# A linear-attention and balanced-expert kernel: the first units in another order, gate weights later in the load queue, and one expert's weight sums behind an addition

## The chip, the cores and the metric

The kernel runs on one NeuronCore of a Trainium2 chip. The metric is the device time of one execution in microseconds (us). Before the change the median of six runs is 411.55 us, from 409.94 to 413.15.

The engines are named as in the profile: PE is TensorE (PEld its weight loads), DVE is VectorE, ACT is ScalarE, POOL is GpSimd, and SP is SyncE, which here only issues transfers.

## The reference

Two blocks follow each other. The first is a linear attention with a decaying state, over 4 sequences, 8 heads, 768 steps and a head size of 48:

```python
for t in range(S):
    kt, vt, rt = (k[:, :, t], v[:, :, t], r[:, :, t])
    cur = np.einsum('bhd,bhe->bhde', u[None] * kt, vt)
    y[:, :, t] = np.einsum('bhd,bhde->bhe', rt, state + cur)
    state = w[None, :, :, None] * state + np.einsum('bhd,bhe->bhde', kt, vt)
```

Its output, as 3072 rows of 384, goes into a layer of 8 experts. Pairs of a token and an expert are taken in falling order of their logits; a pair counts if the token is still free and the expert has fewer than 384 tokens. Each token then goes through its one expert:

```python
logits = x @ w_gate
...
for e in range(E):
    mask = assigned == e
    h = np.maximum(x[mask] @ w1[e], 0.0)      # w1[e]: 384 x 1024
    out[mask] = h @ w2[e]                     # w2[e]: 1024 x 384
```

## The kernel before, in words

**Attention.** The 24 units are pairs of a sequence and a chunk of 128 steps, in chunk order. A unit loads three tensors of 192 KB (`load`, L426: keys `kt`, receptances `rt`, values `vt`), each as 192-byte rows, through SP's queue. Then, for each unit: POOL multiplies `rt` by `kt` and by `u` (`step_products`, L445 and L446); DVE sums that per head into `dd` (`own`, L449), and scales the keys by a table of powers of the decay, `wk`, into `ks` (`scale`, L435); PE transposes receptances and keys (`rows_turned` L461, `keys_turned` L472); DVE scales the turned receptances out of PSUM (`receptances`, L466) and ACT copies the turned keys (L474); PE forms the products of all pairs of steps (`pairs`, L522). The matrix `AT` of a head has `dd` on its diagonal, written by ACT as the identity times a column of `dd` (`diagonal`, L454, one instruction for each of 8 heads), and DVE writes the products above the diagonal over it, under a mask (L524). PE then makes the state's share (L540), the state's update (L550), and the output from `AT` and the values (L567); ACT copies the output (L571). After every fourth unit PE forms the logits (L584), which need the gate weights `wg_sb`.

The first chunk (units 0 to 3) has no state share. Tables and the first two units are made in `Mild.__init__`, ahead of a branch: if all decays lie in a range, `attention_mild` runs, else `attention_any`, which does not run for these inputs. The order of PE, DVE, ACT and POOL there is the order of the code (`manual_schedule`), and inside `attention_mild` that of SP too. So a step that waits holds all later ones of its engine. `wait(n)` (L353) issues products of the identity that nobody reads.

POOL, DVE and PE also carry small constants for the search in the gaps of the units: `constants()` is a generator, and from unit 3 on three of its steps run in each unit.

**Experts.** For each expert a search on DVE, with counts on PE, finds the 384 tokens; POOL gathers their rows (L1238), SP loads `w1` and `w2` (1.5 MB each; L1229, L1284). If the search fails, a longer one (`surely`) runs in a branch at L939; it does not run here. PE forms the hidden layer (L1328), the last 128 rows of the result directly (`result`, L1386), and the first 256 rows by seven products in place of eight (`results`, L1407). For these, DVE makes four sums of quarters of `w2` (`halves_of`, T0 to T3, L1374) and four sums of the hidden layer (L1397 to L1400). The seven products leave PSUM through DVE: `both`, `low`, the second row block's right half (L1422), `high`, then L1426, L1427 and L1430. PSUM has two banks for these products, so the fourth group, p4, waits until `high` has read the second.

In the experts the scheduler of the compiler orders DVE, by its own model of times. With `issue_after(x)` a block's instructions come behind `x` on its engine.

Of the kernel before, what the change touches and what calls it, by code (L numbers as in the profile page):

```python
# [285 lines left out]
class Mild:  # L286
# [6 lines left out]
    def __init__(self, ctx, tc, r, k, v, w, u, wg, ident):  # L293
# [36 lines left out]
        self.load(2)  # L330
        self.wg_sb = const.tile([128, HP, 32], F32, name="wg_sb")
        nc.gpsimd.memset(self.wg_sb, 0.0)
        for i in range(2):
            for j in range(2):
                nc.sync.dma_start(self.wg_sb[i * PD:i * PD + D, j::2, 0:E],
                                  wg.rearrange("(g i j d) e -> i j d g e", i=2, j=2, d=D)[i, j])
        self.load(3)

        self.state = [const.tile([128, HP, PD], F32, name=f"state{b}") for b in range(B)]
# [6 lines left out]
        with part, tc.manual_schedule(engines={nc.tensor.engine, nc.vector.engine, nc.scalar.engine, nc.gpsimd.engine}):  # L346
            awake = part.enter_context(tc.tile_pool(name="m_awake", bufs=1, space=PSUM)).tile([128, 3, 128], F32,
                                                                                              name="awake")

            def wait(n):  # L350

                for _ in range(n):
                    nc.tensor.matmul(awake, ident, ident.unsqueeze(1).to_broadcast([128, 3, 128]),  # L353
                                     start=True, stop=True)


            wait(1)
            row = row.rearrange("p h d -> p (h d)")
            w_ps = ps.tile([128, HP], F32, name="w_ps", tag="kT_ps")
            for a in range(HP):  # L360
                nc.tensor.transpose(w_ps[:, a:a + 1], row[:, ts(a, 128)], ident[0:1, 0:1])
            wait(2)
            wp = const.tile([128, 8, 2, HP], F32, name="wp")
            pw = tab.tile([128, 2, HP, M + 2], F32, name="pw")
            nc.vector.memset(pw[:, :, :, 0:1], 1.0)
            ones = tab.tile([128, 1], F32, name="ones")
            nc.vector.memset(ones, 1.0)

            nc.vector.tensor_scalar(out=wp[:, 0, 0, :], in0=w_ps, scalar1=W_MIN, scalar2=W_MAX,
                                    op0=ALU.max, op1=ALU.min)  # L370
            nc.vector.reciprocal(wp[:, 0, 1, :], wp[:, 0, 0, :])
            for j in range(7):
                n = 1 << j
                m = min(2 * n, M + 2) - n
                by = wp[:, j, :, :].unsqueeze(3).to_broadcast([128, 2, HP, m])
                nc.vector.tensor_mul(pw[:, :, :, n:n + m], pw[:, :, :, 0:m], by)
                nc.vector.tensor_mul(wp[:, j + 1, :, :], wp[:, j, :, :], wp[:, j, :, :])
            self.w_chunk = wp[:, 7, 0, :]

            ch = tab.tile([128, HP, T], F32, name="ch")  # L380
            nc.scalar.copy(ch[:, :, 0:M + 1], pw[:, 0, :, M::-1])
            nc.gpsimd.tensor_copy(ch[:, :, M + 1:T], pw[:, 1, :, 1:T - M])
            self.wr = const.tile([128, HP, T], F32, name="wr")
            nc.scalar.copy(self.wr[:, :, 0:M + 1], pw[:, 1, :, M + 1:0:-1])

            within = tab.tile([128, HP], F32, name="within")
            nc.vector.tensor_tensor(out=within, in0=wp[:, 0, 0, :], in1=w_ps, op=ALU.is_equal)
            nc.vector.tensor_copy(self.wr[:, :, M + 1:T], pw[:, 0, :, 0:T - M - 1])
            self.rows_turned(0)
            wait(1)  # L390
            sc_ps = ps.tile([128, HP, 128], F32, name="sc_ps", tag="kT_ps")
            for a in range(HP):
                nc.tensor.transpose(sc_ps[:, a, :], ch[:, a, :], ident)
            n_ps = awake[0:1, 0, 0:HP]
            nc.tensor.matmul(n_ps, ones, within, start=True, stop=True)
            n_within = tab.tile([1, 1], F32, name="n_within")
            nc.vector.tensor_reduce(out=n_within, in_=n_ps, axis=AX.X, op=ALU.add)
            flag = const.tile([1, 1], I32, name="flag")
            nc.vector.tensor_single_scalar(out=flag, in_=n_within, scalar=float(H * PD), op=ALU.is_equal)
            self.wk = const.tile([128, DX], F32, name="wk")  # L400
            nc.scalar.copy(self.wk.rearrange("p (h d) -> p h d", h=H),
                           sc_ps.rearrange("p a (q d) -> p (a q) d", q=2)[:, :, 0:D])
            self.step_products(0)
            self.receptances(0)
            self.rows_turned(1)
            wait(1)
            self.scale(0)
            self.own(0)
            self.diagonal(0, 0, 2)
            self.keys_turned(0)  # L410
            self.diagonal(0, 2)
            self.step_products(1)
            self.scale(1)
            self.receptances(1)
            self.keys_turned(1)
            self.own(1)
            self.holds = nc.values_load(flag[0:1, 0:1])

    def load(self, n):
# [28 lines left out]
    def own(self, n):  # L448
        self.tc.nc.vector.tensor_reduce(out=self.live[n]["dd"], in_=self.live[n]["rk"], axis=AX.X, op=ALU.add)  # L449

    def diagonal(self, n, first=0, end=None):
        AT, dd = self.live[n]["AT"], self.live[n]["dd"]
        for h in range(first, end or self.r.shape[1]):
            self.tc.nc.scalar.activation(AT[:, h % 2, h // 2, :], self.ident, AF.Copy, scale=dd[:, h:h + 1])  # L454

    def rows_turned(self, n):
# [20 lines left out]
def attention_mild(ctx, tc, mild, r, k, v, w, u, wg, x_dram, LG, ident, walk, first):  # L477
# [141 lines left out]
    search = walk.constants()  # L619
    with tc.manual_schedule(engines={nc.tensor.engine, nc.scalar.engine}):  # L620
        with tc.manual_schedule(engines={nc.vector.engine, nc.gpsimd.engine, nc.sync.engine}):

            nc.tensor.matmul(kv_ps, state[0][:, 0:2, :].rearrange("p a d -> p (a d)"),
                             ident.unsqueeze(1).to_broadcast([128, HP, T]), start=True, stop=True)
            mild.step_products(2)
            mild.scale(2)
            pairs(0)
            mild.diagonal(1)
            mild.own(2)
            for n in range(N):  # L630
                if n + 2 < N:
# [4 lines left out]
                    mild.scale(n + 3)  # L636
                    mild.step_products(n + 3)
                if n + 2 < N:
                    mild.diagonal(n + 2, 0, 4)
                if n + 1 < N:  # L640
                    pairs(n + 1)
                if n > 0 and n % B == 0:
                    logits(n // B - 1)
                if n + 2 < N:
                    mild.diagonal(n + 2, 4)
                from_state(n)
                new_state(n)
                if n > 0 and n % B == 0:
# [35 lines left out]
class Assignment:  # L684
# [26 lines left out]
    def __init__(self, ctx, tc, ML, CAP):  # L711
# [29 lines left out]
        new("own_lo", [128, 1])  # L741
        new("iota_lo", [128, 128], I32)
        new("digits", [128, ND], I32)
        new("steps", [128, 8, ND], I32)
        new("top", [128, ND], I32)
        new("taken", [128, NT])
        new("last", [128, 1])

# [6 lines left out]
    def constants(self):  # L755
# [69 lines left out]
        yield  # L825

        nc.gpsimd.iota(self.digits, pattern=[[1, ND]], base=1, channel_multiplier=0)
        yield
        for g in range(8):
            nc.vector.tensor_single_scalar(out=self.steps[:, g, :], in_=self.digits, scalar=28 - 4 * g,  # L830
                                           op=ALU.logical_shift_left)
            yield

        nc.vector.tensor_single_scalar(out=self.top[:, 0:7], in_=self.steps[:, 0, 0:7], scalar=-1,
                                       op=ALU.bitwise_xor)
        yield
        nc.vector.tensor_single_scalar(out=self.top[:, 7:ND - 1], in_=self.steps[:, 0, 7:ND - 1],
                                       scalar=-2147483648, op=ALU.bitwise_xor)
        yield
        nc.vector.tensor_copy(self.top[:, ND - 1:ND], self.top[:, ND - 2:ND - 1])  # L840
        yield
        nc.gpsimd.memset(self.taken, 0.0)
        yield
# [202 lines left out]
    def surely(self, pool, fmax, acc, place):  # L1046
# [11 lines left out]
        prop = pool.tile([128, NT, E], BF16, name="prop")  # L1058
        tt(prop, self.by_expert(self.first_e), self.by_token(em), ALU.is_equal)


        cand, bits = self.top, None
        for g in range(8):
            all_ps = self.count(pool, m, prop, cand.bitcast(F32), self.digit_15)
            most = pool.tile([128, ND], F32, name="most")
# [14 lines left out]
            if g < 7:  # L1080

                base = pool.tile([128, ND], I32, name="base")
                tt(base, self.steps[:, g + 1, :], flip.to_broadcast([128, ND]), ALU.bitwise_xor)
                cand = pool.tile([128, ND], I32, name="cand")
                nc.vector.scalar_tensor_tensor(out=cand, in0=dg.to_broadcast([128, ND]), scalar=28 - 4 * g,
                                               in1=base, op0=ALU.logical_shift_left, op1=ALU.bitwise_xor)
# [102 lines left out]
def rwkv5_eagle_then_base_layer_balanced(  # L1189
# [202 lines left out]
    def results(n, hid, weights, tok, turn):  # L1392
# [16 lines left out]

        def sum_of(product, other, name):  # L1410
            out = spool.tile([128, HX], F32, name=name)
            nc.vector.tensor_add(out, product, other)  # L1412
            return out

        out = [opool.tile([128, DX], F32, name="o_sb") for _ in range(2)]
        p1, p6 = pair((A[0][0], B[0][0]), (S[1], T[1]))
        one = spool.tile([128, HX], F32, name="one")
# [11 lines left out]
        p4, = pair((A[1][1], T[3]))  # L1429
        nc.vector.tensor_add(out[1][:, 0:HX], p4, low)  # L1430
        store(n, 1, out[1], tok)
        return xT


    awake = ps_t.tile([128, KD, 128], F32, name="xT_ps")
# [3 lines left out]
    for n in range(E):  # L1439
# [9 lines left out]

            ahead = following(n + 2 == E, chain(opening(hid, at, xT), result(n, 2, hid, at["w2"], at["tok"])), late)  # L1450
        else:
            weights_2 = halves_of(at["w2"])
            walk.behind = hidden(hid, 0, at["w1"], xT)
            if n + 1 < E:
                ahead = following(n + 2 == E)
# [1 line left out]
                hidden(hid, j, at["w1"], xT)  # L1457
            for _ in result(n, 2, hid, at["w2"], at["tok"]):
                pass
        xT = results(n, hid, weights_2, at["tok"], lambda: turn(ahead["xg"]) if n + 1 < E else None)  # L1460


# [26 lines left out]
```

## Time and profile before

| | |
|---|---|
| median of 6 runs | 411.55 us |
| profiled execution, time | 412.63 us |
| profiled execution, span of the trace | 410.9 us |
| granted PE clock over the span | 0.998 |
| PE busy | 392.5 us (96%) |
| DVE busy | 264.6 us (64%) |
| ACT busy | 148.2 us (36%) |
| POOL busy | 116.1 us (28%) |

The profiled execution took 412.63 us, 1.7 us more than the span that the trace covers and 1.1 us more than the median. The stages in the trace: tables and the first units' preparation to about 16 us, the units of the attention to 114 us, the last logits, the first search and the first loads to about 142 us, and the eight experts to the end. A line of the timeline gives start and duration in us, engine, line, operation, output and inputs, shape and count; behind it, in brackets, how long the engine was idle before and what ended that.

### The profile page before, as it was taken

The page shows a single profiled execution, that of the slowest core. Times are in us where ns is not written, and L with a number is a line of the kernel's source. Part 1 is how long each engine was busy: PE and PEld are TensorE (multiplying, and loading weights), DVE is VectorE, ACT ScalarE, POOL GpSimd, SP SyncE. Part 2 cuts the span into 40 slices and gives each one's busy share as a digit, 9 for nine tenths or more (in the row PEclk, how much of TensorE's full clock was granted, in tenths as well). Part 3 has the DMA queues.
Part 4 walks back from the last instruction along what each step waited for, and adds up shares of the span by engine and source line. Part 5 has one row for each costly group of instructions (what it writes and reads, how often), then busy time and mean ns, then how long its engine had stood idle before and what let it go on. Part 6 is the DMA issues. An engine that isn't in the chain of part 4 may idle for free. (4 is left out here: it accounts for less than half of the span.)

```text
span 410.9 us, 8511 instructions
## 1 busy us (share of the span) xinstructions
PE 392.5 (96%) x3174; PEld 289.7 (70%) x3174; DVE 264.6 (64%) x777; ACT 148.2 (36%) x382; POOL 116.1 (28%) x154
## 2 busy tenths in 40 slices
PE   7899999999997899989999999999999999999993
PEld 4588888888876495855785685595586577587583
DVE  5798879998568358478568658856856837421021
ACT  3798878778746021202112112121121211202200
POOL 5564964556200201210420320211112032201001
PEclk9999999999999999999999999999999999999999
DMA  9999999740029564712820830641461488201001
GB/s 148 168 173 183 180 177 172 144 76 2 3 78 345 184 230 158 230 38 53 295 77 3 273 125 25 206 180 39 172 213 40 140 304 288 57 21 38 0 21 38
DMA packets 93996, 54.43 MB, mean 132 GB/s; under 512 B 76784, under 2 KB 88176, under 8 KB 93936
## 3 DMA queue, kind: packets, MB, share of 16 engines
q1 hardware_dynamic: 89280, 41.70, 41.0%
q0 software_dynamic: 3072, 9.44, 6.9%
q10 hardware_dynamic: 1584, 2.56, 1.8%
q8 instruction: 29, 0.48, 0.5%
q14 instruction: 31, 0.25, 0.2%
HBM read 44.25 MB, written 9.44 MB: 131 GB/s over the span
## 5 line engine op out<-in xcount | busy, mean ns | idle before, releaser
L1328 PE MATMUL h_ps<-xT,w 128*128 128x384 f32 (+1 forms) x372 | 121.8, 475 | 0.0
L1328 PEld LDWEIGHTS h_ps<-xT,w 128*128 128x128 f32 x372 | 64.6, 190 | 35.9 <-issue 4.0
L1335 ACT ACTIVATE hid<-h_ps 128x384 f32<-128x384 f32 x56 | 27.5, 490 | 115.4 <-PE h_ps L1328 101.9
L1238 POOL DMA_INDIRECT xg<-x_rows,tok x24 | 24.9, 1039 | 144.0 <-issue 121.0
L454 ACT ACTIVATE AT<-ident,dd 128x128 f32<-128x128 f32 x192 | 59.4, 391 | 2.3 <-DVE dd L449 2.3
L1378 POOL DMA_INDIRECT out_dram<-o_sb,tok x24 | 25.9, 1078 | 106.0 <-DVE o_sb L1427 55.4
L1386 PE MATMUL o_ps<-w,hid 128*128 128x384 f32 x128 | 44.4, 493 | 0.9
L524 DVE COPY_PREDICATED AT<-mask,g_ps 128x512 f32<-128x512 uint8 x48 | 32.5, 729 | 8.2 <-PE g_ps L522 8.2
L1386 PEld LDWEIGHTS o_ps<-w,hid 128*128 128x128 f32 x128 | 23.5, 190 | 18.5 <-issue 4.4
L1407 PE MATMUL o_ps<-T,S 128*128 128x192 f32 x192 | 32.5, 326 | 0.0
L1407 PEld LDWEIGHTS o_ps<-T,S 128*128 128x128 f32 x192 | 31.4, 190 | 0.0
L522 PE MATMUL g_ps<-rT,kT 48*128 48x128 f32 x384 | 28.4, 285 | 0.1
L445 POOL TENSOR_TENSOR rk<-rt,kt 128x384 f32<-128x384 f32 x24 | 24.8, 1035 | 8.6 <-DMA rt<-in_r_dram 5.4
L522 PEld LDWEIGHTS g_ps<-rT,kT 48*128 48x128 f32 x384 | 23.6, 187 | 4.9 <-issue 2.9
L446 POOL TENSOR_TENSOR rk<-rk,u_bc 128x384 f32<-128x384 f32 x24 | 26.4, 1099 | 1.9
L567 PE MATMUL y_ps<-AT,vt 128*64 128x128 f32 x368 | 24.6, 276 | 0.0
L1407 PE MATMUL o_ps<-w,hid 128*128 128x192 f32 x128 | 24.6, 326 | 0.0
L1318 ACT COPY xT<-xT_ps 128x384 f32<-128x384 f32 x24 | 10.8, 481 | 34.3 <-PE xT_ps L1317 24.9
L1407 PEld LDWEIGHTS o_ps<-w,hid 128*128 128x128 f32 x128 | 20.9, 190 | 2.1
L1412 DVE TENSOR_TENSOR both<-o_ps,one 128x192 f32<-128x192 f32 x8 | 2.9, 358 | 27.8 <-ACT one L1418 27.8
L567 PEld LDWEIGHTS y_ps<-AT,vt 128*64 128x64 f32 x368 | 19.7, 137 | 0.9 <-issue 0.3
L466 DVE TENSOR_TENSOR rT<-rT_ps,wr 128x512 f32<-128x512 f32 x24 | 16.4, 683 | 5.3 <-PE rT_ps L461 5.2
(240 smaller groups left out, 591.9 us busy)
## 6 DMA issues: line engine op xcount, KB each, us to landing
w<-in_moe_w_dram SPq DMA_DIRECT2D x14, 1536.0 KB, 7.2
kt<-in_k_dram SPq DMA_DIRECT2D x24, 192.0 KB, 4.2
rt<-in_r_dram SPq DMA_DIRECT2D x24, 192.0 KB, 4.8
vt<-in_v_dram SPq DMA_DIRECT2D x24, 192.0 KB, 4.6
x_rows<-AT SPq DMA_DIRECT2D x8, 192.0 KB, 2.9
w<-in_moe_w_dram ACTq DMA_DIRECT2D x1, 1536.0 KB
x_rows<-rt SPq DMA_DIRECT2D x6, 192.0 KB, 2.3
x_rows<-ks SPq DMA_DIRECT2D x5, 192.0 KB, 2.2
```

Of the source, the lines that this page charges most:

```text
L445: nc.gpsimd.tensor_mul(rk, rt[:, :, 0:D], kt)
L446: nc.gpsimd.tensor_mul(rk, rk, self.u_bc.rearrange("p (h d) -> p h d", h=H))
L454: self.tc.nc.scalar.activation(AT[:, h % 2, h // 2, :], self.ident, AF.Copy, scale=dd[:, h:h + 1])
L522: nc.tensor.matmul(g_pss[q][:, a, :], kT[heads[q], a, :], rT[heads[q], a, :], start=True, stop=True)
L524: nc.vector.copy_predicated(out=AT[:, q], mask=mask.unsqueeze(1).to_broadcast([128, HP, T]), data=g_pss[q])
L567: nc.tensor.matmul(y[j][halves[i], g, :], vt[:, 2 * a + j, :], AT[:, j, a, :], start=(c == 0 and g == 0), stop=(g == 1), skip_group_check= ...
L1238: nc.gpsimd.indirect_dma_start(out=xg[:, c, :], out_offset=None, in_=x_dram, in_offset=bass.IndirectOffsetOnAxis(ap=tok[:, c:c + 1], axis=0))
L1328: product = nc.tensor.matmul(h_ps[:, cols], w1[:, f, ts(j, 128)], xT[:, f, cols], start=(f == 0), stop=(f == KD - 1))
L1335: nc.scalar.activation(hid[:, j, :], h_ps, AF.Relu)
L1378: nc.gpsimd.indirect_dma_start(out=out_rows[n * NC + c], out_offset=bass.IndirectOffsetOnAxis(ap=tok[:, c:c + 1], axis=0), in_=o_sb, in_of ...
L1386: nc.tensor.matmul(o_ps, hid[:, j, ts(c, 128)], w2[:, j, :], start=(j == 0), stop=(j == KF - 1))
L1407: nc.tensor.matmul(part, a[:, j, :], b[:, j, :], start=(j == 0), stop=(j == HF - 1))
```

## The change

1. The four transfers of the gate weights (L335) are issued behind the loads of units 4 and 5, and so behind those of units 0 to 5, where they stood behind those of units 0 to 2.
2. In the preparation, one filler ahead of the table's transposes (L390) goes. Receptances of unit 0 come ahead of the flag's two small DVE steps. A filler stands behind the flag's product. Keys of unit 0 are turned ahead of the rows of unit 1. Of unit 0's eight diagonals ACT writes the four of even heads, two before and two after the keys of unit 1; the four of odd heads are written by one DVE product of the identity and `dd`.
3. In `attention_mild` the pairs of unit 0 come ahead of the filler into `kv_ps` (L623) and not behind it.
4. Eleven small DVE steps that make `steps` and `top` go from `constants()` into `surely`.
5. The four sums of the second expert's `w2` are put behind `high` of the first expert.

```diff
@@ Mild.__init__
-        for i in range(2):
-            for j in range(2):
-                nc.sync.dma_start(self.wg_sb[...], wg...)
         self.load(3)
...
             self.rows_turned(0)
-            wait(1)
             sc_ps = ...                      # four transposes of ch
             nc.tensor.matmul(n_ps, ones, within, start=True, stop=True)
-            n_within = ...; flag = ...
             self.wk = ...                    # ACT copy of sc_ps
             self.step_products(0)
             self.receptances(0)
+            n_within = ...; flag = ...
+            wait(1)
+            self.scale(0)
+            self.keys_turned(0)
+            self.own(0)
             self.rows_turned(1)
             wait(1)
-            self.scale(0)
-            self.own(0)
-            self.diagonal(0, 0, 2)
-            self.keys_turned(0)
-            self.diagonal(0, 2)
             self.step_products(1)
             self.scale(1)
+            self.diagonal(0, range(0, H // 2, 2))
             self.receptances(1)
             self.keys_turned(1)
+            self.diagonal(0, range(H // 2, H, 2))
+            live = self.live[0]
+            nc.vector.tensor_mul(live["AT"][:, 1], ident.unsqueeze(1).to_broadcast([128, HP, T]),
+                                 live["dd"][:, 1::2].unsqueeze(2).to_broadcast([128, HP, T]))
             self.own(1)
+            for i in range(2):
+                for j in range(2):
+                    nc.sync.dma_start(self.wg_sb[...], wg...)
@@ attention_mild
-            nc.tensor.matmul(kv_ps, ...)     # the filler
             mild.step_products(2)
             mild.scale(2)
             pairs(0)
+            nc.tensor.matmul(kv_ps, ...)
             mild.diagonal(1, range(H))
@@ Assignment.constants -> Assignment.surely
-        for g in range(8):
-            nc.vector.tensor_single_scalar(out=self.steps[:, g, :], ...)
-        ...                                  # and three steps for top
@@ results / the experts' loop
-            nc.vector.tensor_add(out, product, other)
+            added.append(nc.vector.tensor_add(out, product, other).ins)
...
-            weights_2 = halves_of(at["w2"])
+            with ExitStack() as order:
+                if n == 1:
+                    order.enter_context(tc.issue_after(added))
+                weights_2 = halves_of(at["w2"])
...
-        xT = results(n, hid, weights_2, ...)
+        xT, added = results(n, hid, weights_2, ...)      # added: the add that writes high
```

## The prediction

> **What bounds the kernel now.** I read the page, then the table by stretches, then the timelines of PE and DVE where PE is not full, then the chain of waits.
>
> In the table by stretches the columns are stretch, length, and busy time (instructions) of PE, PEld, DVE, ACT and POOL, then clock, DMA share and GB/s.
>
> ```profile
> 9.90:15.70 5.80, 3.65 (x19) 1.84 (x18) 4.56 (x9) 3.49 (x11) 4.16 (x4) 1.00 1.11 155
> ...
> 15.70:114.10 98.40, 98.33 (x1719) 82.52 (x1719) 83.96 (x161) 80.70 (x234) 55.59 (x79) 1.00 0.76 125
> ...
> 177.40:402.72 225.32, 224.43 (x1008) 156.05 (x1009) 129.63 (x420) 41.06 (x88) 40.99 (x39) 1.00 0.35 119
> ```
>
> From unit 0's pairs at 15.70 to the attention's end, and from 177.40 to the last products, PE runs without a gap. What starts these stretches earlier ends the kernel earlier, as long as operands keep up. Ahead of the first, PE is idle 2.15 of 5.80 us; the timeline of PE shows why:
>
> ```profile
> 7.65 1.49 PE L353 MATMUL awake<-ident 128*128 128x384 f32 x2
> 8.93 0.96 PE L393 MATMUL sc_ps<-ident,ch 128*128 128x128 f32 x4
> 9.82 0.19 PE L395 MATMUL awake<-within,ones 128*1 128x4 f32 x2
> 11.07 0.63 PE L461 MATMUL rT_ps<-ident,rt 128*128 128x128 f32 x4 [1.06 <-issue]
> 11.54 0.81 PE L353 MATMUL awake<-ident 128*128 128x384 f32 x2
> 12.25 0.66 PE L472 MATMUL kT_ps<-ident,ks 128*128 128x128 f32 x4
> 13.90 0.66 PE L472 MATMUL kT_ps<-ident,ks 128*128 128x128 f32 x4 [1.00 <-ACT kT L474]
> 14.65 1.12 PE L623 MATMUL kv_ps<-ident,state 128*128 128x512 f32 x2
> 15.70 1.16 PE L522 MATMUL g_ps<-rT,kT 48*128 48x128 f32 x16
> ```
>
> A filler holds back the table's transposes; PE then waits for DVE, whose timeline is:
>
> ```profile
> 10.30 0.67 DVE L466 TENSOR_TENSOR rT<-rT_ps,wr 128x512 f32<-128x512 f32 x1
> 10.90 1.29 DVE L435 TENSOR_TENSOR ks<-kt,wk 128x384 f32<-128x384 f32 x1
> 12.12 0.54 DVE L449 TENSOR_REDUCE dd<-rk 128x8 f32<-128x384 f32 x1
> 12.58 0.54 DVE L435 TENSOR_TENSOR ks<-kt,wk 128x384 f32<-128x384 f32 x1
> ```
>
> The receptances stand behind the flag, though their operands were there at 8.2; the first key scaling takes 1.29 us where the next takes 0.54, because POOL's product of 10.78 to 11.78 runs beside it.
>
> The second gap is in the list of waits and in the DVE timeline of the first expert's end:
>
> ```profile
> PE o_ps L1407 <- DVE high L1412: 1.3, 1, 1.3
> ```
>
> ```profile
> 174.71 0.96 DVE L1374 TENSOR_TENSOR T<-w 128x768 f32<-128x768 f32 x1 [4.20 <-DMA w<-in_moe_w_dram]
> 175.59 0.35 DVE L1412 TENSOR_TENSOR low<-o_ps,both 128x192 f32<-128x192 f32 x1
> 175.85 0.95 DVE L1374 TENSOR_TENSOR T<-w,T 128x768 f32<-128x768 f32 x1
> 176.72 0.35 DVE L1422 TENSOR_TENSOR o_sb<-o_ps,low 128x192 f32<-128x192 f32 x1
> 176.99 0.35 DVE L1412 TENSOR_TENSOR high<-o_ps,both 128x192 f32<-128x192 f32 x1
> ```
>
> DVE stands 4.20 us behind a sum that waits for the second expert's w2, with `low` and `high` behind it, and PE waits for `high`.
>
> **The preparation.** Without the first filler the table's transposes follow unit 0's rows: L393 moves from 8.93 to 7.85 (7.65, where the filler stood, plus a weight load of 0.2; `ch` is written by 7.55). ACT's copy of the table (0.48, was 9.93) then ends at 9.35. DVE: receptances 8.2 to 8.9, the flag's two steps to 9.3, the key scaling at 9.4. POOL's next product starts at 9.71, when unit 1's `rt` has landed, so the scaling should take 0.54 and end at 9.95. This is the closest race of the change: 0.3 us. Lost, it ends at 11.1 (10.71, where that product ends, plus 0.4).
>
> PE: the new filler writes the bank from which the flag is read, so it waits for that read (9.15), and takes 9.2 to about 10.4 (7.65 to 8.93 before: 1.28). Keys of unit 0 at 10.4, rows of unit 1 at 10.9, a filler at 11.4, keys of unit 1 at 12.05 (steps of 0.49, 0.49 and 0.66), pairs of unit 0 at 12.8 to 12.9 (13.90 to 14.65 is 0.75 between the same places, the branch in it). Queued behind the new wait are only these; the scaled keys of unit 0 (9.95) and 1 (11.4, behind POOL's product and ahead of its next) are there in time. So the pairs start 2.8 us earlier.
>
> The filler at L623 now stands behind them and costs its 1.05 us (14.65 to 15.70) there; in return the second pairs need not wait for the first masked writes: from 17.81 to 19.45 they took 1.64 us, against 1.09 for the first. DVE: the odd diagonals are a product of 512 elements; the 384 of L435 take 0.54 alone and the 512 of L466 0.67, so 0.67 alone and at most 1.0 more behind POOL; DVE itself cannot gain by it, since nothing of DVE's went. I take 0.67 and a wait to 12.4, the end of POOL's product: 13.0. Then `own` to 13.5, unit 2's scaling behind POOL's product of 13.06 to 14.07, so to 14.5, masked writes 14.5 to 15.85. PE wants the second pairs at 12.9 + 1.09 + 1.05 + 0.49 + 0.49 = 16.0. No wait. Sum: 2.8 - 1.05 + 0.55 = **2.3 us**. ACT loses four activations of 0.3 each and stays ahead.
>
> Bounds: 1.4 if the race is lost; 2.6 if the new filler runs at the full clock. The clock: PE's steps shorten between 9.8 and 11.1 us, after PE had run from 4.07 on (L461 takes 1.06 at 6.79 and 0.63 at 11.07), and gaps of 1.06 and 1.00 afterwards did not lengthen them again (0.66 for the same four at 13.90). PE's work from 4.07 to 10 becomes no thinner, so I set nothing for it. The Trainium skill (TensorE: Matmul & The Clock Gate, "The HAM clock gate") puts the grant at the end of a busy, free-running window of about 3.4 us: were a window missed for the removed filler, by that page some 1.7 us would be lost, as an estimate.
>
> **The loads.** SP issues nine loads of units 3 to 5 without the 2.40 us of L335 between them, and the lull (18 GB/s from 13 to 14 us) goes. Loads land about 1.13 us apart (`kt` 8.35, 11.7: 3.4 per unit), so unit 3's `rt` lands at about 16.2, not 17.15, unit 5's at about 23.1, not 24.5. The units need 3.5 us each on PE (L571 at 24.86, 28.36, 31.86), so they do not outrun this. The four gate transfers now delay unit 6: SP is through with unit 5 at about 20 (21.7 before), plus 2.4, plus 0.86 for the branch, so 23.3 against 22.59, and `rt` of unit 6 lands at about 28.1 (27.36). PE turns it at 31.34 - 2.3 = 29.0. Cover 0.9 us; beyond it each us costs PE one, at most 1.5. The gate weights themselves land by 26 and are first needed at 33.45 - 2.3 = 31.1.
>
> DVE has 3.5 us of work in a unit, so a collision with POOL (up to 0.75, row L435) can push it behind PE, but the masked writes have 0.7 us before PE wants their bank, and the logits' units are 5.5 us long. I set nothing, with 0.5 in the range. The Trainium skill (SBUF — State Buffer, on the shared port pair) has DVE operations with two SBUF inputs and POOL lock each other out for a whole instruction, whichever starts first; by that rule one more DVE product of this kind speaks against the change, with at most one POOL product, an estimate of 1 us, where DVE is the one that PE waits for.
>
> **The eleven constants.** Their rows are 4.0 us of DVE (L830 2.70, then 0.98, 0.18, 0.15), between 76.8 and 91. PE's units there are 4.10 us as elsewhere (L571 at 76.65, 80.78, 84.87), so it is worth nothing while PE covers it. They lengthen the seven jumped blocks at L939, whose join stops DVE 0.33 to 0.35 us, and 3.19 the first time. DVE idles 2.73 before `both`; a longer fetch is hidden there up to that.
>
> **The second expert's sums.** Compare with the next expert, where the sums stand behind `high`: first product of `results` to the first hidden product is 201.33 to 211.55, 10.22 us, here 167.00 to 178.79, 11.79. So **1.57 us**; at least the 1.30 of the wait. `low` comes 2.25 after `both` (204.48 to 206.73), so 172.4, and `high` ends at 173.4, ahead of PE's wish for its bank (175.9). The sums still start at 174.71, when w2 lands; four of 0.95 and three additions fill DVE to about 179.4, and the next count, on PE's heels, comes at 181.27 - 1.57 = 179.7. A few tenths later are hidden, because the gather behind that search lands some 3 us before PE's turn at 206.53.
>
> **Sum.** 2.3 + 1.57 = 3.9. The profiled 412.63 (span 410.9 and 1.7 around it) becomes 408.7; it stood 1.1 above the median, so the median goes from 411.55 to **407.7 us**. Here 0.3% is 1.2 us, about the least that a measurement of this kernel tells from none.
>
> **The rivals.**
> - *The preparation's gain is cut*: race lost (-0.9), unit 6 late, or DVE behind in units 1 to 3 (0.5 to 1). For it: 0.3 us of race, 0.9 of cover. Against: they do not add up, a late PE has more cover. 408.5 to 409.9, middle 409.
> - *It is swallowed*: the loads, at 3.4 us per unit, set the pace and return all 2.3. Against: PE's unit is 3.5, later 4.1. 411.55 - 1.57 = 410.0.
> - *The edge does nothing new*: the scheduler puts something else in front of `high`. 411.55 - 2.3 = 409.25. Against: in six experts `high` follows `low` at once.
> - *Slower*: the compiler's scheduler, with other times in its model, puts the weight sums ahead of `low` in later experts as it did in the second; only that one gets the edge. Each costs 1.57. From three experts on (4.7 against 3.9) the kernel is slower; with all six 407.7 + 9.4 = 417.1. For it: it happened once. Against: six experts in one order, and w2 there was asked for long before.
>
> **How the numbers follow.** Forecast 0.62 (406.9 to 408.4 by the bounds), cut gain 0.20, swallowed 0.04, no effect of the edge 0.04, slower rival 0.07; 0.03 for mishaps that cancel. The range from 406.8 to 410.2 leaves out the slower rival and some tails. Faster 0.88, same 0.04, slower 0.08.
>
> **What would show it.** Right: L522 first at about 12.9; the first L550 at about 17.1 (19.45); PE without gaps after; the last L571 of the attention at about 111.8 (114.10); no wait of PE for `high`, and 10.2 us for the first `results`. Wrong: the first L435 above 1 us, PE idle before L461 of unit 6 with a DMA as releaser, DVE waiting for w in front of `low` in any expert, or L472 first at over 0.9 us for its four.

## The result, and the profile after

The changed kernel takes 409.24 us in the median of 20 runs (408.70 to 412.03), beside 411.46 us for the kernel before in the runs taken with it. The ratio is 0.995, with a 95% interval of 0.9936 to 0.9964: 2.1 us saved by the ratio, by its interval 1.5 to 2.6. The forecast was 407.7 us, that is 3.9 us saved. The measured median lies inside the stated range of 406.8 to 410.2, but above the forecast's own bounds (406.9 to 408.4): it falls where the rival of a cut gain stood (408.5 to 409.9), to which the prediction gave 0.20. The profiled execution took 409.06 us (span 407.4); the forecast's sum had put it at 408.7.

The table by stretches of the changed kernel, with the same columns as before. Its line numbers: fillers L349, table L388, flag's product L390, flag L397, odd diagonals L414, scaling L439, rows L465, keys L476, pairs L526, filler into `kv_ps` L630, state products L554.

```profile
8.60:13.07 4.47, 3.29 (x19) 2.04 (x19) 4.41 (x8) 1.68 (x5) 4.08 (x5) 1.00 1.06 211
13.07:111.82 98.75, 98.75 (x1720) 82.61 (x1721) 81.63 (x153) 81.43 (x236) 58.02 (x80) 1.00 0.64 126
173.99:399.15 225.16, 224.31 (x1010) 155.95 (x1009) 129.32 (x420) 41.15 (x88) 41.47 (x39) 1.00 0.34 119
```

The two full stretches are as long as before (98.75 against 98.40 us, with 0.35 more at its start; 225.16 against 225.32). They start 2.63 and 3.41 us earlier. In the stretch ahead of the first, PE is still idle 1.18 of 4.47 us. PE's timeline shows where:

```profile
7.93 0.74 PE L388 MATMUL sc_ps<-ident,ch 128*128 128x128 f32 x4
8.61 0.19 PE L390 MATMUL awake<-within,ones 128*1 128x4 f32 x2
9.43 0.91 PE L349 MATMUL awake<-ident 128*128 128x384 f32 x2 [0.63 <-DVE n_within L397]
10.84 0.66 PE L476 MATMUL kT_ps<-ident,ks 128*128 128x128 f32 x4 [0.50 <-DVE ks L439]
...
12.41 0.60 PE L476 MATMUL kT_ps<-ident,ks 128*128 128x128 f32 x4
13.07 1.16 PE L526 MATMUL g_ps<-rT,kT 48*128 48x128 f32 x16
14.16 1.13 PE L630 MATMUL kv_ps<-ident,state 128*128 128x512 f32 x2
15.12 0.60 PE L465 MATMUL rT_ps<-ident,rt 128*128 128x128 f32 x4
15.56 0.60 PE L476 MATMUL kT_ps<-ident,ks 128*128 128x128 f32 x4
16.09 1.16 PE L526 MATMUL g_ps<-rT,kT 48*128 48x128 f32 x16
```

The new filler waits 0.63 us for the flag's read of its bank, and keys of unit 0 wait 0.50 us for their scaling. From 10.84 on there is no gap. The timelines of DVE and of POOL at that place:

```profile
9.48 1.30 DVE L439 TENSOR_TENSOR ks<-kt,wk 128x384 f32<-128x384 f32 x1
```

```profile
9.37 1.00 POOL L449 TENSOR_TENSOR rk<-rt,kt 128x384 f32<-128x384 f32 x1
```

POOL started 0.11 us ahead of DVE, and the scaling took 1.30 us: the race is lost in this execution. A first L435 above 1 us was one of the forecast's signs of being wrong.

At the second gap PE's wait for `high` is gone from the list of waits. The timeline of DVE at the first expert's end:

```profile
165.25 0.36 DVE L879 TENSOR_TENSOR dead<-acc,fe 128x192 uint8<-128x192 bf16 x1 [1.53 <-issue]
...
170.47 0.36 DVE L1412 TENSOR_TENSOR low<-o_ps,both 128x192 f32<-128x192 f32 x1 [1.54 <-PE o_ps L1407]
170.86 0.36 DVE L1423 TENSOR_TENSOR o_sb<-o_ps,low 128x192 f32<-128x192 f32 x1
171.14 0.34 DVE L1412 TENSOR_TENSOR high<-o_ps,both 128x192 f32<-128x192 f32 x1
171.84 1.82 DVE L1374 TENSOR_TENSOR T<-w 128x768 f32<-128x768 f32 x2 [0.35 <-DMA w<-in_moe_w_dram]
```

The sums of `w2` (L1374) now stand behind `high`, as meant. The first row is new: DVE stands still for 1.53 us with no operand missing ("issue"), three steps behind the join of the block that is jumped (the longer search, which does not run), and ahead of the sums of the hidden layer that PE's second group needs.

### The profile page after: what moved, and what is told of

It reads as the page before. It is cut to its first block, busy times and chain, and to the rows that moved or that the text cites. A ratio compares the mean times of both kernels' runs of the same rounds, so it can differ in the third digit from the quotient of the medians.

```text
span 407.4 us, 8503 instructions
## 1 busy us (share of the span) xinstructions
PE 390.9 (96%) x3174; PEld 289.0 (71%) x3174; DVE 262.3 (64%) x767; ACT 147.2 (36%) x378; POOL 118.3 (29%) x154
## 5 line engine op out<-in xcount | busy, mean ns | idle before, releaser
L458 ACT ACTIVATE AT<-ident,dd 128x128 f32<-128x128 f32 x188 | 58.1, 392 | 0.0
L526 PE MATMUL g_ps<-rT,kT 48*128 48x128 f32 x384 | 27.9, 285 | 0.1
L526 PEld LDWEIGHTS g_ps<-rT,kT 48*128 48x128 f32 x384 | 23.3, 187 | 4.1 <-issue 2.9
```

The source lines that it names most:

```text
L526: nc.tensor.matmul(g_pss[q][:, a, :], kT[heads[q], a, :], rT[heads[q], a, :], start=True, stop=True)
```

## The experiments

All times are medians. The kernel before was measured with each group: 412.22 us with the first four, 411.58 with the next four, 411.67 with the last four. The marks of all profiles stand in one table behind the experiments.

### The two halves apart

The edge alone: the kernel before, with part 5 only.

```diff
+            with ExitStack() as order:
+                if n == 1:
+                    order.enter_context(tc.issue_after(added))
+                weights_2 = halves_of(at["w2"])
```

> The kernel before with part 5 alone (the second expert's four sums behind the fourth addition). Theory A, that the gap at the first expert's end is the same in every execution: 1.3 to 1.6 us faster than before, about 410.0. Theory B, that the gap depends on when w2 lands and the profiled execution of before had a long one: 0.3 to 0.8 us faster, about 411. Both: no wait of PE for high in the profile, results of the first expert in 10.2 to 10.5 us.

Measured: 410.84 us, ratio 0.9959 (0.9939 to 0.9978), so 1.4 us saved by the medians and 1.7 by the ratio (by its interval 0.9 to 2.5). The first `results` take 10.22 us (166.18 to 176.40 in PE's timeline), to the hundredth what the next expert takes. The edge does what the forecast said.

All but the edge: the changed kernel without those lines.

> The changed kernel without part 5. Theory A: 1.3 to 1.6 us slower than the changed kernel, so 410.5 to 410.8, and the profile shows PE waiting about 1.3 us for high again. Theory B: 409.5 to 410.0, with a wait whose length follows the landing of w2. The preparation's gain by this run: 0.7 to 1.0 us under A, 1.5 to 2.0 under B.

Measured: 410.19 us, ratio 0.9953 (0.9936 to 0.997): 2.0 us saved. In its list of waits stand both the wait that the edge removes and a new one:

```profile
PE o_ps L1407 <- DVE high L1412: 0.7, 1, 0.7
...
PE o_ps L1407 <- DVE S L1399: 0.3, 1, 0.3
```

The kernel before and the changed kernel, each once more in the same group:

> The kernel before, once more, for a second profile of it. Time 411.5 within 0.3. Theory A: PE waits 1.3 us for high again and the first pairs start at 15.7. Theory B: another length of that wait (0 to 2 us), by another landing of w2. Theory C, that the granted clock's start moves the preparation: the first pairs start more than 0.5 us from 15.7 when the clock is granted at another time than 10.0.

> The changed kernel once more, for a second profile of it. Time 409.2 within 0.3. The attention's last full copy (111.82 in the first profile) within 0.3 us under A and B; under theory C it moves by as much as the grant of the clock does, up to 1.7 us.

Measured: 412.18 us (ratio 1.0019, 0.9991 to 1.0046) and 409.47 us (0.9939, 0.9921 to 0.9958). The halves sum to 3.4 us, both together gave 2.75; the intervals do not tell this difference from none. What the repeats are worth is their profiles. In the second profile of the kernel before, the first state products start at 18.82 us and not at 19.45, and the list of waits has the second gap shorter than the 1.3 us of the first profile:

```profile
PE o_ps L1407 <- DVE high L1412: 1.0, 1, 1.0
```

With 1.3 and 1.0 us in the kernel before and 0.7 us in the changed kernel without the edge, this wait is not the same in every execution: DVE's wait for `w2` was 4.20, 3.86 and 3.27 us in these three. Beside the changed kernel of the same group (409.47) the edge is worth 0.7 us. So the gap is not the same in every execution, as theory B has it, though the edge alone brought theory A's 1.4 us. The timeline of DVE in the second profile has a further difference:

```profile
10.71 0.56 DVE L435 TENSOR_TENSOR ks<-kt,wk 128x384 f32<-128x384 f32 x1
```

The kernel before runs the same race with POOL's product, and its first scaling, which took 1.29 us in the first profile, won it here.

So the profile that the forecast read was late by 0.63 us in the preparation and long by 0.34 us at the edge (11.79 against 11.45 us for the first `results`). These are the two places that the change shortens.

The second profile of the changed kernel took 411.11 us. Its preparation and first `results` are those of the first; the loss is late, in the list of the eighth expert's tokens. PE's and DVE's timelines there:

```profile
349.51 0.18 PE L1177 MATMUL list_ps<-part,alike 128*128 128x12 f16 x1 [1.84 <-DVE part L1175]
```

```profile
347.36 0.96 DVE L1374 TENSOR_TENSOR T<-w 128x768 f32<-128x768 f32 x1 [2.44 <-DMA w<-in_moe_w_dram]
```

The eighth expert's sums of `w2` wait for their transfer, and `part`, for which PE waits, stands behind them on DVE: the same fault as the one that the edge mends, in another expert.

### The constants back in the attention

The changed kernel with part 4 undone: `steps` and `top` are kept in the search's constants again and made in the attention's gaps.

```diff
+        new("steps", [128, 8, ND], I32)
+        new("top", [128, ND], I32)
...
+        for g in range(8):
+            nc.vector.tensor_single_scalar(out=self.steps[:, g, :], ...)
+            yield
```

> The changed kernel with the eleven constants back in the gaps of the attention. Theory A (they are hidden in the attention, and their move shifted DVE's instruction stream, so that DVE stops for 1.5 to 1.75 us with no operand missing in front of the first expert's results, which delays the sums of the hidden layer): the stop is gone, the first results take 10.2 us (10.45 and 10.69 in the two profiles of the changed kernel), nothing is longer in the attention, and the kernel is 0.2 to 0.5 us faster than the changed one. Rival (the stop belongs to the edge or to the new order of the first units, and the constants cost the attention something): the stop stays, first results 10.45 to 10.7, and the last attention copy comes up to 0.4 later.

Measured: 409.52 us, ratio 0.9955 (0.993 to 0.998), no different from the changed kernel. Theory A holds for the stop: it is gone, and the first `results` take 10.22 us. But the attention is 1.5 us longer (first state products to last copy 96.15 us, 94.64 in the changed kernel), and the last copy comes 0.89 us later (112.71 against 111.82), where theory A had nothing and the rival up to 0.4 us. PE's timeline at unit 6 has a wait that the changed kernel has not:

```profile
29.95 0.63 PE L465 MATMUL rT_ps<-ident,rt 128*128 128x128 f32 x4 [0.94 <-DMA rt<-in_r_dram]
```

The race of the preparation was won here (the first scaling took 0.56 us): `rt` of unit 1 landed so late that POOL started at 10.01. First pairs stand at 12.44 us.

### POOL held behind the first scaling

```diff
+            behind = const.tile([128, 1], F32, name="behind")
+            nc.gpsimd.tensor_copy(behind, self.live[0]["ks"][:, 0, 0:1])
             self.step_products(1)
```

> The changed kernel with a one-column copy on POOL that reads unit 0's scaled keys, ahead of unit 1's products, so that POOL cannot start before DVE's first key scaling has ended. Theory A (the lost race is what the preparation lacks against the forecast): the scaling takes 0.54 us and ends at about 10.0, keys of unit 0 are turned at 10.3 to 10.4 in place of 10.84, first pairs at 12.3 to 12.4 in place of 12.8 to 13.07, and everything after is 0.4 to 0.5 us earlier. Rival (the delay moves on: DVE's next scaling now meets POOL's later products, and DVE reaches the masked writes no earlier): first pairs 12.3 to 12.9, but the first state products (17.2 to 17.3 in the changed kernel) no more than 0.1 us earlier.

Measured: 408.64 us (408.37 to 409.09), ratio 0.9924 (0.9899 to 0.9949). In the timelines of DVE, POOL and PE (lines are two further down):

```profile
9.27 0.56 DVE L441 TENSOR_TENSOR ks<-kt,wk 128x384 f32<-128x384 f32 x1
```

```profile
9.89 0.19 POOL L407 COPY behind<-ks 128x1 f32<-128x1 f32 x1 [0.78 <-DVE ks L441]
10.03 1.01 POOL L451 TENSOR_TENSOR rk<-rt,kt 128x384 f32<-128x384 f32 x1
```

```profile
12.50 1.16 PE L528 MATMUL g_ps<-rT,kT 48*128 48x128 f32 x16 [0.27 <-PE kT_ps L478]
...
16.61 0.56 PE L556 MATMUL kv_ps<-vt,ks 128*48 128x48 f32 x16
```

Theory A: the first state products come 0.57 us earlier than in the changed kernel's profile (17.18), and the median is 0.6 lower than the changed kernel's 409.24, which was measured in another group. That is the price of the lost race in that profile; the forecast had 0.9.

### The kv_ps product in the place of the early filler

```diff
-            wait(1)
+            nc.tensor.matmul(self.kv_ps, self.state[0]..., ident..., start=True, stop=True)
             self.scale(0)
...
             pairs(0)
-            nc.tensor.matmul(kv_ps, ...)
```

> The changed kernel with the product that fills kv_ps put where the filler behind the flag's product stood, in a bank that no flag step reads, and none behind the first pairs (the branch that does not run gets one PSUM bank less). Theory A (PE carries the time between the first and the second pairs): the first state products come 1.05 to 1.1 us earlier after the first pairs, about 3.0 us in place of 4.1, and the kernel is about 1 us faster. Rival (DVE carries it: the second pairs wait for the masked writes, which end at 16.0 behind the odd diagonals, a head sum and a scaling): PE waits for DVE ahead of the second pairs, the first state products come at 17.0 to 17.2 as now, and the kernel is at most 0.2 us faster.

Measured: 410.16 us, ratio 0.9964 (0.995 to 0.9979). PE's and DVE's timelines between the first and the second pairs:

```profile
12.78 1.16 PE L528 MATMUL g_ps<-rT,kT 48*128 48x128 f32 x16
...
15.19 1.76 PE L528 MATMUL g_ps<-rT,kT 48*128 48x128 f32 x16
16.88 0.56 PE L556 MATMUL kv_ps<-vt,ks 128*48 128x48 f32 x16
```

```profile
13.58 0.89 DVE L441 TENSOR_TENSOR ks<-kt,wk 128x384 f32<-128x384 f32 x1
14.39 1.35 DVE L530 COPY_PREDICATED AT<-mask,g_ps 128x512 f32<-128x512 uint8 x2
```

The filler's 1.1 us is gone, and first pairs to first state products still take 4.10 us, against 4.11. The second pairs start earlier and stretch from 1.16 to 1.76 us, because their second bank is read by DVE's masked write until 15.7. The rival is right: DVE carries here, and PE's filler was free. The median is higher than the changed kernel's, not lower: this profile needs 53.75 us from the last attention copy to the first `results`, 0.7 more than the changed kernel's, around the fillers behind the branch. Why is open; and as the profiled execution took 409.40 us, the least of the twelve runs, it can show only a part of what the median lost.

Both edits together:

> The two edits before together: POOL's product held behind the first scaling, and the kv_ps product in place of the early filler. Theory A (PE alone carries): the two gains add, first state products at about 15.7, the kernel about 1.5 us faster than the changed one. Rival (DVE carries from 12 us on): DVE's chain from the first scaling to the masked writes starts 0.7 us earlier and then carries, so the first state products come at 16.4 to 16.8, 0.4 to 0.8 us earlier than in the changed kernel, and more than the first of the two edits alone brings.

Measured: 410.10 us, ratio 0.9953 (0.993 to 0.9976). The first state products come at 16.52 us, in the rival's range: DVE's chain, once started earlier, sets the time. The median is 1.5 us above that of POOL held alone, in the same group. The stretch behind the branch is 0.9 us longer than in the changed kernel here too, and 0.5 longer than with POOL held alone; the rest of the loss is not explained.

### The gate weights back

The four transfers stand between the loads of units 2 and 3 again, all else as in the changed kernel.

> The changed kernel with the first part undone: the four gate transfers are issued between the loads of units 2 and 3 again. Theory A (the place of these transfers is worth nothing at the usual pace of the loads, since PE is covered on both sides): within 0.3 us of the changed kernel, no wait of PE for a load, first state products at 16.9 to 17.3. Rival 1 (the early place holds back unit 3 and PE or POOL waits for its load): PE waits for a transfer ahead of unit 3 or 4, 0.5 to 2 us slower. Rival 2 (the late place costs now and then: one profile here, of a run with slow loads, had PE wait 0.94 us for unit 6's receptances): the runs of this kernel lie closer together, and the median is up to 0.4 us lower.

Measured: 409.34 us (408.43 to 409.86), ratio 0.9932 (0.991 to 0.9955). PE waits for no load, the first state products start at 16.89 us. The median is that of the changed kernel within 0.1 us: as far as six runs tell, the place of these transfers is worth nothing at this pace of the loads.

### Combinations

POOL held, and the constants back:

> The kernel that holds POOL's product behind the first key scaling, with the eleven constants back in the attention's gaps as well. Theory A (the constants are hidden there, and their move is what makes DVE stop ahead of the first results): first results 10.2 us in place of 10.54, the units of the attention as long as before (94.64 us from the first state products to the last copy), and 0.3 us faster than the same kernel without this edit (0.9924 of the time of before). Rival (it is the edit's place in the code that shifts a stop from one spot to another): first results 10.2 us, but another stop appears, and the time is within 0.2 us or worse.

Measured: 409.61 us (409.32 to 411.68), ratio 0.9952 (0.9929 to 0.9976). Without the constants it was 408.64, in another group, so theory A fails and the rival holds. POOL held, and the eighth expert's sums behind `high` too:

```diff
-                if n == 1:
+                if n in (1, E - 1):
```

> The kernel that holds POOL's product behind the first key scaling, with the eighth expert's sums of second weights behind the fourth addition as the second's are. In one profile of the changed kernel these sums waited 2.44 us for their weights, and the eighth expert's list stood behind them on DVE, so PE waited 1.84 us for it; in another 0.71 us and none. Theory A: no PE wait for the list beyond the two of 0.55 us in the first searches, first both to last both 193.5 us in every run, and the median 0 to 0.5 us lower with a shorter upper tail. Rival (the sums are wanted earlier in their new place, or fill DVE when PE wants a bank): the last expert's products wait for DVE, 0.3 to 1 us slower.

Measured: **408.51 us** (408.36 to 408.64), ratio 0.9917 (0.9896 to 0.9938), the lowest of all. The list of the eighth expert does not wait, and the second expert's `both` to the last takes 193.29 us, the lowest but one. It is only 0.13 us below POOL held alone, the runs of the two overlap, and that kernel's profile has no wait for this list either, so what the second edge is worth is not shown. All three:

> All three: POOL's product held, constants back in the attention, both edges. Theory A (the effects add): first state products at 16.6, first results 10.2 us, first both to last both 193.5 us: 0.3 to 0.8 us faster than the kernel that only holds POOL's product, so about 407.8 to 408.3 where before is 411.6. Rival (a stop moved by the code's layout takes it back): no faster than the better of the two edits alone.

Measured: 409.32 us (408.90 to 411.06), ratio 0.994 (0.9919 to 0.9961), in the same group as the one before: the effects do not add, and keeping the constants costs 0.8 us. In both kernels that keep them the first `results` take the clean 10.22 us and the attention is 0.7 and 1.0 us longer, with unit 6 late again. PE's timeline of the first and of the second:

```profile
29.54 0.63 PE L467 MATMUL rT_ps<-ident,rt 128*128 128x128 f32 x4 [0.63 <-DVE state L564]
```

```profile
29.84 0.63 PE L467 MATMUL rT_ps<-ident,rt 128*128 128x128 f32 x4 [0.91 <-DMA rt<-in_r_dram]
```

The first is put down to a step of DVE that has nothing to do with `rt`; POOL's product of the same `rt` starts at 29.56, so I read it as the transfer too. So I compared the loads of all profiles. Here is SP's transfer queue from 4 to 16 us: packets, MB, and the time of the packets as a share of 16 engines' 12 us, of the kernel before, the changed one, and the two with the constants back (without, and with POOL held):

```profile
q1 hardware_dynamic: 11338, 2.07, 127.1%
```

```profile
q1 hardware_dynamic: 13851, 2.62, 109.9%
```

```profile
q1 hardware_dynamic: 11734, 2.22, 138.1%
```

```profile
q1 hardware_dynamic: 11704, 2.21, 142.8%
```

One packet took 21.5 ns before (127.1% of 16 times 12 us, over 11338), 15.2 ns after, and 22.6 and 23.4 ns with the constants kept. In the whole of the loads (4 to 84 us) 18 to 24% of the 192-byte packets took 24 ns or more in the six profiles of kernels that keep `steps` and `top`, and 0.8 to 0.9% in the eight of kernels that do not. By the queue's share from 4 to 16 us a packet took 19.5 to 23.4 ns in the six and 15.1 to 15.5 ns in the eight. At 4 to 16 us not one of the constants' steps has run, since they begin in unit 3. What differs by then is where the tiles lie: `steps` and `top` take 512 and 64 bytes of each partition, and the tiles of the loads, allocated behind them, lie 576 bytes lower without them. In the compiled programs `rt` of unit 0 starts at byte 56704 of each partition before, and at 56128 after.

### The marks of all profiles

In us, from the timelines: start of the first state products; from there to the last attention copy; from there to the first `results`; first `results` to the next hidden products; second expert's `both` to the last one.

| kernel | first state products | attention | to results | results | both to both | median |
|---|---|---|---|---|---|---|
| before | 19.45 | 94.65 | 52.90 | 11.79 | 193.59 | 411.46 |
| before again | 18.82 | 94.64 | 52.96 | 11.45 | 194.15 | 412.18 |
| edge alone | 18.69 | 94.64 | 52.85 | 10.22 | 193.75 | 410.84 |
| all but the edge | 16.91 | 94.63 | 52.98 | 11.76 | 193.67 | 410.19 |
| changed | 17.18 | 94.64 | 53.02 | 10.45 | 193.51 | 409.24 |
| changed again | 17.28 | 94.64 | 52.96 | 10.69 | 195.29 | 409.47 |
| constants back | 16.56 | 96.15 | 52.98 | 10.22 | 194.00 | 409.52 |
| POOL held | 16.61 | 94.64 | 53.47 | 10.54 | 193.57 | 408.64 |
| kv_ps early | 16.88 | 94.64 | 53.75 | 10.38 | 193.50 | 410.16 |
| both of these | 16.52 | 94.64 | 53.95 | 10.48 | 193.54 | 410.10 |
| gate early | 16.89 | 94.64 | 54.08 | 10.28 | 193.71 | 409.34 |
| held, constants back | 16.95 | 95.34 | 53.19 | 10.22 | 193.66 | 409.61 |
| held, last edge | 16.79 | 94.64 | 53.14 | 10.48 | 193.29 | 408.51 |
| all three | 16.98 | 95.61 | 53.35 | 10.22 | 193.28 | 409.32 |

## Why the prediction was right, and where its steps failed

**Direction and places: right.** Both gaps closed where the forecast said, and in the changed kernel's profile nothing of it was given back later: from the second expert's `both` to the last 193.51 us, against 193.59.

**The anchor: the step that failed.** The sum of 3.9 us was made against the profiled execution, and there it nearly holds: 412.63 - 3.9 = 408.7, and the changed kernel's profile reads 409.06. The forecast then took the same 3.9 off the median, because the profile "stood 1.1 above the median". That excess was no offset common to both kernels. Against the second profile of before, 0.63 us of it lay in the preparation and 0.34 in the wait for `w2` behind which `high` stood, that is, in the two gaps themselves. (The second profile lost 0.56 us elsewhere: 194.15 against 193.59 us from `both` to the last.) A run without the excess has that much less to gain.

**The terms, from more than one profile.** Preparation: forecast 2.3. Against the first profile 19.45 - 17.18 = 2.27; against the other two of the old order (18.82 and 18.69) 1.5 to 1.6. The first profile was late where its own race was lost and its clock late: one of the others won the race (0.56 us), and in the other PE's full clock came at 7.92 us, not at 9.66. Edge: forecast 1.57. In the kernel before it brought 11.45 - 10.22 = 1.23 to 1.57; in the changed kernel 11.76 - 10.69 = 1.07 to 11.76 - 10.45 = 1.31. Sum with typical profiles 2.6 to 2.9, measured 2.2 and 2.75.

**The preparation, step by step.** Table at 7.93 (7.85), first pairs at 13.07 and 12.80 (12.8 to 12.9), first state products at 17.18 (17.1), last copy at 111.82 (111.8). Yet the race, which these figures take as won, was lost in both profiles of the changed kernel (1.30 and 1.29 us). So it is in part luck that these marks came out: other steps were earlier, the new filler among them (0.91 us for 1.28, since the full clock had begun), and a loss costs less than the forecast's 0.9 us. The first state products start at 16.52 to 16.98 us where POOL is held, and at 16.88 to 17.28 in the kernels of the new order that do not hold it and lost, so a loss costs 0.8 us at most, and nothing in some pairs of profiles. Of "-1.05 + 0.55" the sum is right and the reading is not: the filler costs nothing by itself, DVE's chain through the odd diagonals, a head sum, unit 2's scaling and the masked writes needs the same 4.1 us.

**The lock and the clock.** The same product on DVE took 1.30 us when POOL had started first, and 0.56 us in the second profile of the kernel before, where DVE started at 10.71 us and POOL at 10.93; there POOL's product took 1.19 us in place of 1.00. The Trainium skill (SBUF — State Buffer, on the shared port pair) gives the pair to whichever of two such products starts first, and blocks the other; by their order these rows agree. The full granted clock began at 9.66 and 9.26 us in the two profiles of the kernel before, and at 8.18 and 7.75 in the two of the changed one; in the ten others it began between 6.93 and 9.63 us. So no profile shows that the removed filler cost one of the windows of about 3.4 us that the Trainium skill (TensorE: Matmul & The Clock Gate, "The HAM clock gate") tells of.

**The loads: right outcome, wrong reason.** The forecast put `rt` of unit 6 at 28.1 us, 0.9 ahead of PE. In the three kernels with the new order and the constants kept, unit 6's rows start at 29.95, 29.54 and 29.84 us, after a wait of 0.63 to 0.94: the rival of a cut gain, as it stood in the text. In the changed kernel POOL took the same `rt` at 25.95 us (27.36 in its second profile), and all its loads ran faster.

**The constants: the step sized at zero.** They are worth nothing as work on DVE, as said (the attention takes 94.64 to 94.65 us with them in the three profiles of the old order, and 94.64 without). Their move did two other things. With it the loads ran faster. The whole move is worth 0.8 us by the pair of kernels that differ in it alone and were measured together (408.51 and 409.32); in the pairs from different groups it is 1.0 us with POOL held (408.64 and 409.61) and at most 0.3 without (409.24 and 409.52). And it lengthened the jumped blocks, as the forecast said, but the price was looked for in the wrong place. The forecast hid a longer fetch in DVE's 2.73 us of idle time before `both`. The sums of the hidden layer stand between the join and `both`, and PE wants them first. In all eight profiles with the longer block DVE stops for 1.35 to 1.80 us, two to four steps behind that join, and the first `results` take 10.28 to 10.69 us with the edge; in all six with the shorter one there is no such stop, and 10.22 us with the edge. The edge fell short by 0.23 and 0.47 us in the two profiles of the changed kernel for this reason.

**What stays open.** That the place of the tiles is what slows the packets is argued from the two groups of profiles, not shown: no run moves the tiles alone. The Trainium skill (DMA: Bandwidth & Descriptors, "How a descriptor splits into AXI transactions") says that the first transaction of a descriptor that does not start at a multiple of 256 bytes starts at the boundary below it; it tells this of reads, and here rows are written. Rows of 192 bytes at steps of 256 would cross such a boundary with the old start (56704 is 128 above a multiple of 256) and just reach it with the new one (56128 is 64 above). Taken over to writes, the rule would make every packet of `rt` slow before, where a fifth to a quarter of all were, and half of those of `kt`, whose rows stand at steps of 192 bytes, before and after, where under 1% were slow after; so it fits in sign and not in size. That DVE's stop is a fetch of instructions is argued from its place and from the length of the block, and no run takes the block alone; why the later joins show 0.33 to 0.36 us in both kernels is open. So is the stretch from the last copy to the first `results`, which varies from 52.85 to 54.08 us, and the loss of median with the kv_ps product moved.

## What to carry to other kernels

Before a sum is taken off a median, ask where the profile's excess over the median lies: if it lies in the gap that the change closes, it is part of the gain and must not be counted again. Where a scheduler has put a step that waits for a transfer in front of one that PE waits for, look for the same fault in all other rounds of the loop: here it stood in the eighth expert too, and mending both, with POOL held back where it blocked DVE, gave 408.51 us, the lowest median here. A tile that is dropped can move the tiles behind it, as here by 576 bytes, so compare the time per packet of the loads before and after any change of the allocation.

## What the hardware showed that was not expected

- The same loads cost 15.1 to 15.5 ns or 19.5 to 23.4 ns per packet from 4 to 16 us; the eight profiles without the two constant tiles stand on one side, the six with them on the other.
- A block of instructions that is jumped and never runs may cost: in the eight profiles with eleven more small steps in it DVE stood for 1.35 to 1.80 us just behind one of its joins, with no operand missing by the profile, and in the six without them it did not. The tiles lie elsewhere too in the eight, so the block alone is not shown to be the cause.
- A busy PE does not say that PE carries: without 1.1 us of filler between the first two pairs, first pairs to first state products took 4.10 us, against 4.11 with it.
